# Fixed order for the exponents and sines on ScalarE in a fused attention, feed-forward and expert kernel

## The chip, the cores and the metric

The kernel runs on one core of a Trainium2 chip. The metric is device time in microseconds (us) of one execution, inputs and outputs in HBM. Before the change the median of three runs is 1149.26 us (1148.4 to 1151.08).

## What is computed

Three stages follow each other, all in float32.

```python
# 1. attention: q, k, v are (4, 8, 768, 64); 4 sink columns, window of 128
scores = scale * (q @ k.T); scores = where(is_sink | in_window, scores, -1e9)
a = exp(scores - rowmax); a = a / (rowsum(a) + 1e-9); x = a @ v     # -> (3072, 512)
# 2. feed-forward: w_in (512, 2048), w_out (2048, 512)
h = x @ w_in; g = h * cos(h); x = g @ w_out
# 3. top-1 of 8 experts, 512 -> 1024 -> 512
logits = x @ w_gate + modality_bias[modality_id]; e = argmax(logits)
out[token] = softmax(logits)[e] * (relu(x @ w1[e]) @ w2[e])
```

Stage 1 takes an exponent of every kept score, stage 2 a cosine of every hidden value (made as a sine with a phase of a quarter turn), and the gate of stage 3 a small exponent for every group of tokens. The hidden values are split into a high and a low part for the matrix products, so most products are made of three matmuls.

## The kernel before, in words

The 3072 tokens are eight groups of 384 (`hb` 0 to 7: half a batch item each). Attention of a group goes over four pairs of heads, so there are 32 pairs in all. `attn_front` (L403) loads and transposes q and k of a pair. `mid` (L485) computes its scores in three tiles of 128 rows (`t` 0 to 2), two heads each: matmuls into a PSUM bank `ps`, then a VectorE operation (L516) that masks, copies to `Pb` and leaves the row's maximum in `mx`. After all six blocks stands a loop of six exponents on ScalarE (L529 to L533), one for each tile and head, that read `mx` and leave the row sums in `sm`. `mid` hands back control after every tile of scores, and once more behind the six exponents; between the six it does not. `rest` (L536) normalises the probabilities (on VectorE from `hb` 3 on, on GpSimd in the groups before), transposes them on TensorE (`pt`, L560 to L570), evicts them (`pT`) and multiplies them with v (`po`).

The feed-forward part (`ffn_tile_gen`, from L656) runs one group behind attention, in 128 chunks: 16 blocks of 128 hidden columns for each of eight groups. A chunk is twelve matmuls `hp` (L691 to L693), two VectorE operations that reduce the angle (L142, L145, tile `ch`), one sine on ScalarE (L702), a product with `hp` on VectorE that also frees its PSUM bank (two banks take turns), a copy `g_h` on ScalarE (L712), the low part `g_l` on GpSimd, and two chunks later nine matmuls `y` (L640). `run_ffn` lets chunks pass in step with the weights that the attention part yields; so in the text of the program a few chunks, with their sines, stand between two pairs and between the tiles of scores of one pair. The first group's chunks are divided: six at the start, ten at the very end. Groups 0 and 1 are piped: there a pair's scores and exponents are issued together with the rest of the pair before it. Groups 2 and up issue a pair's scores, its exponents, the next pair's front, and then its rest.

The program text is not the final order. A planner goes over it before the run, with modelled durations, and fixes for each engine one queue: of the instructions that are ready by its model, the one that stands first in the program. Each engine then runs its queue strictly in that order, waiting on semaphores. ScalarE evaluates exponents and sines from tables, and an `ACT_TABLE_LOAD` is put into its queue, after the order is fixed, wherever the next function needs the other table; copies and ReLU need none. The router's exponents (L787, eight of them) are a third user of tables.

After the last chunk the experts run in grids of 256 tokens, with a queue order written out by hand; no exponent or sine is left there. `add_manual_dep(later, earlier, NoSync)` is used in the kernel already for matmuls (`mmf`, L637): it gives the planner an order and puts no semaphore into the program.

Of the kernel before, what the change touches and what calls it, by code (L numbers as in the profile page):

```python
# [16 lines left out]
AF = mybir.ActivationFunctionType  # L17
# [4 lines left out]
TWO_PI = 2.0 * math.pi  # L22
# [39 lines left out]
def kernel(  # L62
# [39 lines left out]
    PE, ACT, DVE, POOL, SP = nc.tensor, nc.scalar, nc.vector, nc.gpsimd, nc.sync  # L102
# [32 lines left out]
    def mm(o, l, r, start, stop):  # L135
        PE.matmul(o, l, r, start=start, stop=stop)  # L136
# [173 lines left out]
        xT[hb] = (xpool.tile([P, NPAIR, HALF], F32R, name="xT_h"), xpool.tile([P, NPAIR, HALF], F32R, name="xT_l"))  # L310

    fronts = {}

    def steps(hb):
        return STEPS_0 if hb <= 1 else STEPS_1
# [80 lines left out]
    def attn_front(hb, pr):  # L396
# [14 lines left out]
        def psb(name):  # L411
            if hb > 0 or not extra:
                return ps_a(name)
            n_ps[0] += 1
            return ps_y(n_ps[0] % NQ, name)
# [67 lines left out]
        mx = sm = Pb = Pt = cols = None  # L483

        def mid():  # L485
            nonlocal mx, sm, Pb, Pt, cols
            kf = [t.rearrange("p t s -> p (t s)") for t in kT]
            klf = [t.rearrange("p t s -> p (t s)") for t in kl] if stack else None
            if extra:
                Pb = [[pb_x[2 * t + j][:, 0:W3] for j in range(2)] for t in range(NQ)]  # L490
            else:
                Pt = late_pool().tile([P, NQ, 2, W3], F32, name="Pb2") if hb >= PB2 and pr % 2 else apool.tile([P, NQ, 2, W3], F32, name="Pb", bufs=PBB)
                Pb = [[Pt[:, t, j] for j in range(2)] for t in range(NQ)]
            mx = apool.tile([P, 2 * NQ], F32, name="mx", bufs=2)
            sm = apool.tile([P, 2 * NQ], F32, name="sm", bufs=2)

            def cols(t):
                if half == 0:
                    return (SEG, W3, 0) if t == 0 else (0, W3, (t - 1) * SEG)
                return 0, W3, t * SEG  # L500

            def scores(t, js):

                c0, c1, o = cols(t)
                w = c1 - c0
                qs = slice(t * P, (t + 1) * P)
                ps = {j: psb("ps") for j in js}
                for j in js:
                    if stack:
                        mm(ps[j][:, 0:w], qT[j][:, qs], kf[j][:, o:o + w], True, False)  # L510
                        mm(ps[j][:, 0:w], qT[j][:, qs], klf[j][:, o:o + w], False, True)
                    else:
                        mm(ps[j][:, 0:w], qT[0][hr[j], qs], kf[0][hr[j], o:o + w], True, True)
                for j in js:
                    i = 2 * t + j
                    DVE.tensor_tensor_reduce(  # L516
                        out=Pb[t][j][:, c0:c1], in0=ps[j][:, 0:w], in1=masks[:, min(half * NQ + t, 2), c0:c1],
                        scale=-SCALE, scalar=3.0e38, op0=ALU.add, op1=ALU.min, accum_out=mx[:, i:i + 1])

            for t in range(NQ):  # L520
                if hb >= PAIRED:
                    scores(t, (0, 1))
                    yield 2 * steps(hb)[1]
                else:
                    for j in range(2):
                        scores(t, (j,))
                        yield steps(hb)[1]
            for t in range(NQ):
                for j in range(2):  # L529
                    c0, c1, _ = cols(t)  # L530
                    i = 2 * t + j
                    ACT.activation(out=Pb[t][j][:, c0:c1], in_=Pb[t][j][:, c0:c1], func=AF.Exp, scale=-1.0,  # L532
                                   bias=mx[:, i:i + 1], accum_out=sm[:, i:i + 1])  # L533
            yield steps(hb)[2]
        def rest():
            xh, xl = xT[hb]  # L536
# [119 lines left out]
    def span(i):  # L656
        return (F0 if i == NTILE else 0), (F0 if i == 0 else NF)
# [4 lines left out]
    def ffn_tile_gen(ypool_of):  # L662
        LAG = 2
        g_t = {}
        yps = {}

        def second(c):
            i, f = seq[c]
            f0, f1 = span(i)
            if f == f0:  # L670
                yps[i] = [ps_y(tt_, f"y{tt_}") for tt_ in range(NQ)]
            gh, gl = g_t.pop(c)
            oh, ol = wo_h[f], wo_l.pop(c)
            for t in range(NQ):
                yp = yps[i][t]
                s = slice(t * P, (t + 1) * P)
                mmf(yp, gh[:, s], oh, f == f0, False)
                mmf(yp, gh[:, s], ol, False, False)
                mmf(yp, gl[:, s], oh, False, f == f1 - 1)
                yield  # L680

        def load_wo(c):
            if c >= F0:
                wo_l[c] = wo_tile()
                SP.dma_start(out=wo_l[c].bitcast(F32), in_=wl_scr[seq[c][1]])

        for c in range(n_all + LAG):
            if c < n_all:
                i, f = seq[c]

                xh, xl = xT[i]  # L691
                hp = ps_h("hp")[:, 0:HALF]
                for p_ in range(NPAIR):  # L693
                    mm(hp, wi_h[f][:, p_, :], xh[:, p_, :], p_ == 0, False)
                    mm(hp, wi_h[f][:, p_, :], xl[:, p_, :], False, False)
                    mm(hp, wi_l[f][:, p_, :], xh[:, p_, :], False, p_ == NPAIR - 1)
                    if p_ < NPAIR - 1:
                        yield c + 0.125 * (p_ + 1)
                ch = mpool.tile([P, HALF], F32, name="ch", bufs=CHB)
                ts(DVE, ch.bitcast(I32), hp, 1.0 / TWO_PI, ALU.mult, 0.25, ALU.add)  # L700
                stt(DVE, ch, hp, 1.0 / TWO_PI, ch.bitcast(I32), ALU.mult, ALU.subtract)
                ACT.activation(out=ch, in_=ch, func=AF.Sin, scale=TWO_PI, bias=half_pi)  # L702
                yield c + 0.5
            if c >= LAG:
                for n_, _ in enumerate(second(c - LAG)):
                    if n_ < NQ - 1:
                        yield c + 0.5 + (n_ + 1) / 6.0
            if c < n_all:
                tt(DVE, ch, ch, hp, ALU.mult)
                gh = mpool.tile([P, HALF], F32R, name="g_h", bufs=GB)  # L710
                gl = mpool.tile([P, HALF], F32R, name="g_l", bufs=GB)
                ACT.activation(out=gh, in_=ch, func=AF.Copy)  # L712
                tt(POOL, gl, ch, gh.bitcast(F32), ALU.subtract)
                g_t[c] = (gh, gl)
                load_wo(c)
            if c == n_all + LAG - 3:
                for r_ in routes:
                    for _ in r_:
                        pass
                routes.clear()  # L720
                ysb[NTILE] = [ypool_of().tile([P, YC], F32, name="yt", bufs=NQ) for _ in range(NQ)]
                for t in range(NQ):
                    SP.dma_start(out=ysb[NTILE][t][:, 0:DM], in_=yp_scr[t])
            i, f = seq[c - LAG] if c >= LAG else (0, -1)
            if f == span(i)[1] - 1:
                if i == 0:

                    for t in range(NQ):
                        yt = mpool.tile([P, DM], F32, name="y_part", tag="wo_l", bufs=WL_BUFS)
                        ACT.activation(out=yt, in_=yps[0][t], func=AF.Copy)  # L730
                        SP.dma_start(out=yp_scr[t], in_=yt)
                elif i == NTILE:
                    for t in range(NQ):
                        yt = ysb[i][t][:, 0:DM]
                        tt(DVE, yt, yps[i][t], yt, ALU.add)
                    ysb[0] = ysb.pop(NTILE)
                    routes.append(route_tile(0, ypool_of()))
                else:
                    ysb[i] = []
                    for t in range(NQ):  # L740
                        yt = ypool_of().tile([P, YC], F32, name="yt", bufs=NQ)
                        ACT.activation(out=yt[:, 0:DM], in_=yps[i][t], func=AF.Copy)
                        ysb[i].append(yt)
                    routes.append(route_tile(i, ypool_of()))
            yield c + 1.0
# [90 lines left out]
    cst = ExitStack()  # L836
    cpool = cst.enter_context(tc.tile_pool(name="cpool", bufs=1))
    conv = conv_gen(cpool)
    ypl = {}
    late_st = ExitStack()  # L840

# [9 lines left out]
    def late_pool():  # L851
        ypool_of()
        return ypl["late"]
# [43 lines left out]
    prow, half_pi = cols2[:, 0:1], cols2[:, 1:2]  # L897
# [149 lines left out]
    for nm in ("xT_h", "xT_l"):  # L1047
        t = xpool.tile([P, KD, 256], F32R, name="m_" + nm, tag=nm)
# [354 lines left out]
```

## Time and profile before

| | |
|---|---|
| runs | 1149.26 us median (1148.4, 1149.26, 1151.08) |
| the profiled execution | 1149.4 us, of which the traced span is 1147.6 us |
| instructions | 20806 |
| groups 0 and 1, attention almost alone | 0 to about 65 us |
| feed-forward and attention together | about 65 to 680 us |
| feed-forward alone | about 680 to 825 us |
| experts | about 825 us to the end |

The traced span begins with the first instruction and ends with the last; 1.8 us of the execution lie around it. An engine is busy where one of its instructions runs; register, branch, semaphore and DMA-issuing instructions don't count. PE is TensorE's matmuls, PEld its weight loads, which run beside matmuls, DVE is VectorE, ACT ScalarE, POOL GpSimd. Matmuls overlap in the pipeline, so a busy PE is not PE at its peak, and a wait of less than the pipeline's depth doesn't show as idle time.

### The profile page before, as it was taken

What the parts mean: (1) busy time and instruction counts of PE and PEld (TensorE: products, weight loads), DVE (VectorE), ACT (ScalarE), POOL (GpSimd) and SP (SyncE); (2) the same over time, 40 slices, a digit from 0 to 9 for tenths busy, and PEclk for the clock granted to TensorE, in tenths of its full rate; (3) what the DMA queues carried; (4) which work ended last, traced back from release to release, by engine and by line L of the source; (5) the groups of instructions that cost most, each with busy time, mean ns of one, the idle gap of its engine ahead of it and who ended that gap; (6) DMA issues with size and microseconds to landing.
All of it is one profiled execution on the core that took longest, in us unless ns stands there. A gap on an engine that the chain in (4) does not pass through costs nothing.

```text
span 1147.6 us, 20806 instructions
## 1 busy us (share of the span) xinstructions
PE 1093.7 (95%) x6504; PEld 936.0 (82%) x6504; DVE 716.4 (62%) x2206; ACT 629.4 (55%) x1283; POOL 224.8 (20%) x275
## 2 busy tenths in 40 slices
PE   5989999999999999999999999999999998999995
PEld 3667677888888888878888889899889997899994
DVE  6678888877876877886788774746741225622210
ACT  4878887766676676666777553434222225522221
POOL 1232224211111111111111112321112211121110
PEclk9999999999999999999999999999999999999998
DMA  6566666433333433433253223723151115111110
GB/s 149 139 193 197 195 200 168 113 86 84 95 91 83 118 82 75 112 86 83 72 118 96 69 78 107 251 62 111 47 193 53 61 39 184 33 62 41 39 42 24
DMA packets 139286, 118.56 MB, mean 103 GB/s; under 512 B 96367, under 2 KB 105583, under 8 KB 139120
## 3 DMA queue, kind: packets, MB, share of 16 engines
q1 hardware_dynamic: 134800, 103.02, 32.3%
q0 software_dynamic: 4320, 13.65, 3.6%
q8 instruction: 65, 1.06, 0.4%
q14 instruction: 101, 0.83, 0.2%
HBM read 151.06 MB, written 19.67 MB: 149 GB/s over the span
## 4 chain that ended last, share of the span: by engine, by line
PE 76%; DVE 12%; ACT 4%; DMA 4%; issue 2%; POOL 1%; SPq 0%; DVEq 0%; POOLq 0%; ACTq 0%
PE hp L136 19%; PE y L640 18%; PE m_y L136 10%; PE m_h L136 10%; PE po L136 5%; PE ps L136 4%; DMA out_dram<-m_ot,m_ids 3%; PE pl L768 1%; DVE pT L148 1%; DVE qT L148 1%; DVE ch L142 1%; DVE kl L148 1%; PE m_a L1107 1%; PE pq L445 1%; PE pt L570 1%
## 5 line engine op out<-in xcount | busy, mean ns | idle before, releaser
L148 POOL TENSOR_TENSOR g_l<-ch,g_h 128x384 fp32r<-128x384 f32 x128 | 133.4, 1043 | 552.9 <-ACT g_h L712 497.6
L136 PE MATMUL hp<-xT_h,wi_h 128*128 128x384 f32 x512 | 182.2, 356 | 2.7 <-DVE ch L148 2.7
L136 PE MATMUL hp<-xT_l,wi_h 128*128 128x384 f32 x512 | 174.7, 341 | 0.0
L136 PE MATMUL hp<-xT_h,wi_l 128*128 128x384 f32 x512 | 174.1, 340 | 0.0
L640 PE MATMUL y<-wo,g_h 128*128 128x512 f32 x384 | 157.2, 411 | 0.0
L640 PE MATMUL y<-wo_l,g_h 128*128 128x512 f32 x384 | 156.0, 406 | 0.0
L640 PE MATMUL y<-wo,g_l 128*128 128x512 f32 x384 | 154.6, 403 | 0.2 <-POOL g_l L148 0.2
L702 ACT ACTIVATE ch<-ch,cols 128x384 f32<-128x384 f32 x128 | 78.9, 617 | 119.4 <-DVE ch L145 117.6
L136 PE MATMUL m_y<-wi_h,hT 128*128 128x512 f32 x416 | 132.5, 393 | 0.7 <-ACT m_ot L1149 0.5
L145 DVE SCALAR_TENSOR_TENSOR hT<-m_h,hT 128x256 fp32r<-128x256 f32 x88 | 37.4, 425 | 151.9 <-ACTq L1301 94.9
L136 PEld LDWEIGHTS hp<-xT_h,wi_h 128*128 128x128 f32 x512 | 96.8, 189 | 10.7 <-issue 3.4
L136 PEld LDWEIGHTS hp<-xT_l,wi_h 128*128 128x128 f32 x512 | 96.9, 189 | 5.5 <-issue 1.9
L142 DVE TENSOR_SCALAR ch<-hp 128x384 int32<-128x384 f32 x128 | 71.0, 555 | 48.0 <-PE hp L136 36.2
L136 PEld LDWEIGHTS hp<-xT_h,wi_l 128*128 128x128 f32 x512 | 96.5, 189 | 1.2 <-issue 0.9
L712 ACT ACTIVATE g_h<-ch 128x384 fp32r<-128x384 f32 x128 | 66.5, 521 | 54.1 <-DVE ch L148 42.9
L148 DVE TENSOR_TENSOR ch<-ch,hp 128x384 f32<-128x384 f32 x128 | 70.4, 550 | 38.3 <-ACT ch L702 37.9
L136 PEld LDWEIGHTS m_y<-wi_h,hT 128*128 128x128 f32 x416 | 78.0, 188 | 16.9 <-issue 0.9
L532 ACT ACTIVATE Pb<-Pb,mx 128x272 f32<-128x272 f32 (+1 forms) x168 | 83.0, 496 | 9.3 <-DVE mx L516 8.4
L640 PEld LDWEIGHTS y<-wo,g_l 128*128 128x128 f32 x384 | 72.3, 188 | 14.2 <-POOL g_l L148 0.8
L1118 ACT ACTIVATE hT<-m_h 128x256 fp32r<-128x256 f32 x88 | 34.0, 387 | 88.0 <-PE m_h L136 80.9
L136 PE MATMUL m_y<-wi_l,hT 128*128 128x512 f32 x208 | 81.0, 389 | 0.0
L640 PEld LDWEIGHTS y<-wo,g_h 128*128 128x128 f32 x384 | 72.4, 189 | 10.5 <-issue 2.7
(280 smaller groups left out, 2368.1 us busy)
## 6 DMA issues: line engine op xcount, KB each, us to landing
rw<-in_moe_w_dram SPq DMA_DIRECT2D x112, 512.0 KB
wo_l<-wl_scr SPq DMA_DIRECT2D x122, 256.0 KB
cv_in<-in_moe_w_in_dram SPq DMA_DIRECT2D x16, 512.0 KB
cv_out<-in_moe_w_out_dram SPq DMA_DIRECT2D x16, 512.0 KB
y_scr<-yt SPq DMA_DIRECT2D x24, 256.5 KB
xT_h<-xg_h SPq DMA_DIRECT2D x32, 192.0 KB
xT_l<-xg_l SPq DMA_DIRECT2D x32, 192.0 KB
qn<-in_q_dram SPq DMA_DIRECT2D x56, 96.0 KB
```

The costliest lines, as they stand in the source:

```text
L136: PE.matmul(o, l, r, start=start, stop=stop)
L142: e.tensor_scalar(out=o, in0=i, scalar1=s1, scalar2=s2, op0=op0, op1=op1)
L145: e.scalar_tensor_tensor(out=o, in0=i0, scalar=s, in1=i1, op0=op0, op1=op1)
L148: e.tensor_tensor(out=o, in0=a, in1=b, op=op)
L445: PE.transpose(pq[:, t * P:(t + 1) * P], qn[:, t].rearrange("p j d -> p (j d)"), ident)
L532: ACT.activation(out=Pb[t][j][:, c0:c1], in_=Pb[t][j][:, c0:c1], func=AF.Exp, scale=-1.0, bias=mx[:, i:i + 1], accum_out=sm[:, i:i + 1])
L570: PE.transpose(pt[:, j, P:2 * P], Pb[t][j][:, SEG:W3], ident)
L640: i = PE.matmul(o, l, r, start=start, stop=stop)
L702: ACT.activation(out=ch, in_=ch, func=AF.Sin, scale=TWO_PI, bias=half_pi)
L712: ACT.activation(out=gh, in_=ch, func=AF.Copy)
L768: return PE.matmul(pl[0][:, 0:NE], yT[:, c, :], wg[:, c, :], start=c == 0, stop=c == KD - 1)
L1118: ACT.activation(out=hT_h[f], in_=hp, func=AF.Relu)
```

## The change

Each exponent of a pair (L532) and each sine (L702) is given an order edge to the one of them that was issued before it in the program. So the planner keeps them in one row, as the program has them: all six exponents of a pair next to each other, as far as these two functions are concerned, and the sines of the chunks in between where the program has them. Copies, ReLUs and the router's exponents are not in the row and may still be placed anywhere. No semaphore, no instruction and no tile is added.

```diff
     fronts = {}
+    row = [None]
+
+    def in_row(i):
+        if row[0] is not None:
+            tc.add_manual_dep(i.ins, row[0].ins.name, in_order, reason="exponents and sines in the order given")
+        row[0] = i
...
-                    ACT.activation(out=Pb[t][j][:, c0:c1], in_=Pb[t][j][:, c0:c1], func=AF.Exp, scale=-1.0,
-                                   bias=mx[:, i:i + 1], accum_out=sm[:, i:i + 1])
+                    in_row(ACT.activation(out=Pb[t][j][:, c0:c1], in_=Pb[t][j][:, c0:c1], func=AF.Exp, scale=-1.0,
+                                          bias=mx[:, i:i + 1], accum_out=sm[:, i:i + 1]))
...
-                ACT.activation(out=ch, in_=ch, func=AF.Sin, scale=TWO_PI, bias=half_pi)
+                in_row(ACT.activation(out=ch, in_=ch, func=AF.Sin, scale=TWO_PI, bias=half_pi))
...
     conv = conv_gen(cpool)
+    in_order = mybir.DependencyInfo(mybir.DependencyClass.NoSync, mybir.DependencyReason.DATA)
```

## Rows read from the trace of the kernel before

**Rows 1.** Page, part 1: busy us, share of the span, instructions of each engine.
```profile
PE 1093.7 (95%) x6504; PEld 936.0 (82%) x6504; DVE 716.4 (62%) x2206; ACT 629.4 (55%) x1283; POOL 224.8 (20%) x275
```

**Rows 2.** Stretches: width, busy us (instructions) of PE, PEld, DVE, ACT, POOL; clock; DMA.
```profile
65.00:110.00 45.00, 41.85 (x266) 31.45 (x267) 34.72 (x81) 37.89 (x81) 14.18 (x30) 0.96 0.66 189
110.00:680.00 570.00, 555.07 (x3269) 469.76 (x3268) 452.17 (x1419) 401.71 (x789) 112.03 (x125) 1.00 0.41 107
680.00:825.00 145.00, 144.31 (x811) 129.96 (x811) 87.09 (x242) 54.99 (x96) 32.69 (x31) 1.00 0.35 112
```

**Rows 3.** ACT's groups: line, operation, count | busy us, mean ns | idle before, releaser.
```profile
L702 ACT ACT_TABLE_LOAD x52 | 66.7, 1283 | 0.9
L532 ACT ACT_TABLE_LOAD x44 | 56.5, 1283 | 0.8
L787 ACT ACT_TABLE_LOAD x8 | 10.3, 1283 | 0.1
L262 ACT ACT_TABLE_LOAD x1 | 1.3, 1283 | 0.7 <-PEq L1382 0.7
```

**Rows 4.** PE's waits from 110 to 680 us: total us, times, longest.
```profile
PE pt L560 <- DVE pT L148: 3.3, 6, 0.6
...
PE pt L560 <- ACT pT L572: 1.6, 3, 0.6
...
PE pz L592 <- POOL kl L451: 0.2, 1, 0.2
```

**Rows 5.** ACT's timeline, pair 14: start us, duration us, instruction [idle before].
```profile
236.26 1.28 ACT L532 ACT_TABLE_LOAD   x1
237.56 0.53 ACT L532 ACTIVATE Pb<-Pb,mx 128x272 f32<-128x272 f32 x1
238.08 0.51 ACT L532 ACTIVATE Pb<-Pb,mx 128x272 f32<-128x272 f32 x1
...
239.72 1.28 ACT L702 ACT_TABLE_LOAD   x1
241.01 0.62 ACT L702 ACTIVATE ch<-ch,cols 128x384 f32<-128x384 f32 x1
241.65 1.28 ACT L532 ACT_TABLE_LOAD   x1
...
243.46 0.51 ACT L532 ACTIVATE Pb<-Pb,mx 128x272 f32<-128x272 f32 x1
243.88 0.19 ACT L532 ACTIVATION_READ_ACCUMULATOR Pb<-Pb,mx 128x1 f32 x1
```

**Rows 6.** DVE's timeline, pair 14: the angle and the last maximum.
```profile
238.98 0.56 DVE L145 SCALAR_TENSOR_TENSOR ch<-hp,ch 128x384 f32<-128x384 f32 x1
...
240.17 0.08 DVE L516 DVE_READ_ACCUMULATOR2_ANT mx<- 128x1 f32 x1
```

**Rows 7.** PE's timeline behind a split (pair 14) and an unsplit group (pair 18).
```profile
248.84 0.41 PE L560 MATMUL pt<-ident,Pb 128*128 128x128 f32 x2 [0.47 <-DVE pT L148]
...
342.62 0.41 PE L570 MATMUL pt<-ident,Pb 128*128 128x128 f32 x2 [0.17 <-DVE qT L148]
```

**Rows 8.** ACT's timeline, pair 18: the last exponent, then the sine that waits.
```profile
337.00 0.19 ACT L532 ACTIVATION_READ_ACCUMULATOR Pb<-Pb,mx 128x1 f32 x1
337.21 1.28 ACT L702 ACT_TABLE_LOAD   x1
```

**Rows 9.** DVE's timeline, pair 18: the angle of that sine.
```profile
337.37 0.55 DVE L145 SCALAR_TENSOR_TENSOR ch<-hp,ch 128x384 f32<-128x384 f32 x1
```

**Rows 10.** ACT's timeline around the first sine.
```profile
65.16 1.28 ACT L702 ACT_TABLE_LOAD   x1
66.45 1.12 ACT L702 ACTIVATE ch<-ch,cols 128x384 f32<-128x384 f32 x2
```

**Rows 11.** PE's timeline: first matmul behind that sine; first use of pair 6's exponents.
```profile
67.71 0.44 PE L136 MATMUL hp<-xT_h,wi_h 128*128 128x384 f32 x1 [2.73 <-DVE ch L148]
...
80.88 0.33 PE L569 MATMUL pt<-ident,pb_x 128*128 128x128 f32 x1
```

## The prediction

> **What bounds the kernel now.** I read the page's first part, then the busy time by stretch, then who waits for whom, and only then timelines. TensorE is the busiest engine, with its weight loads at 82% of the span, VectorE stands at 62% and ScalarE at 55% [rows 1]. ScalarE's share hides a table bill: 105 table loads of 1.283 us, together 134.8 us of its 629.4 [rows 1, 3]. By stretch, feed-forward alone (680 to 825 us) leaves TensorE idle for 0.7 us, so nothing there can be won. From 65 to 110 us it is idle for 3.15 us, from 110 to 680 us for 570 - 555.07 = 14.9 us, while ScalarE is busy for 84% and 70% of these [rows 2]. Everything that this change can win lies in those 18 us of idle time, and in delays too short to show as idle. Of the 14.9 us, 27 waits of over 0.15 us are named, nearly all of them of one kind: TensorE reaches the transposes `pt` (or `pz`, `po`) of a pair before the engines that prepare them are done [rows 4]. They sum to 14.05 us.
>
> **Why exponents and sines matter to these waits.** Of pair 14 the timeline shows what "split" means: a load, four exponents, a load, one sine, a load, two exponents [rows 5]. I laid all exponents and sines of the trace out in the order in which the program issues them. In each of pairs 9 to 32 one sine stands ahead of the six exponents in the program and runs behind some of them in the trace: the planner saw the exponents ready first and had no price for the two extra loads. In 21 of these 24 pairs the sine splits the group (pair 14 is one), in three (11, 18, 26) it comes behind all six. The 24 waits that follow split groups sum to 13.3 us, 0.63 us a pair; the two behind unsplit ones to 0.34 us, 0.11 us a pair (one of each stands in [rows 7]). A group's exponents can also be late because of VectorE, so this is a comparison of few cases, not a proof.
>
> **The change part by part.**
>
> *Loads.* In program order there are 28 runs of exponents and 28 of sines, which take turns. Three of the router's eight exponents stand beside a run of exponents, four among sines (two loads each), and one is last (one load): 28 + 28 + 8 + 1 = 65 loads, if the router's stay where they are. That takes 40 x 1.283 = 51.3 us from ScalarE [rows 3], which is not on TensorE's path as such. In the timeline the load costs its 1.28 us and nothing more: the sine begins 0.01 us behind its load, and the next load 0.02 us behind the sine [rows 5]. The Trainium skill (ScalarE: Activation LUTs, What ACT_TABLE_LOAD costs) adds a drain of about 1380 ns to each switch. By that figure the three loads of a split group would take about 8.0 us instead of 3.9, an estimate by the page, and the recovery below would go to its far end, 1138.5 us. The trace disagrees with the drain, as the 0.01 us shows.
>
> *The sine comes first.* This is what the change adds, and it is a wait. The sine of pair 14 is ready at 238.98 + 0.56 = 239.54 us, 0.71 us before the last maximum at 240.25 [rows 6]. Today four exponents run while ScalarE waits for it. With the edges all six queue behind it, and behind them on ScalarE whatever copies the planner puts there (`qT`, `kT`, `g_h`, `pT`), for which TensorE and VectorE wait. The table holds sines at that point, so the sine needs no load: it ends 0.04 + 0.62 us after 239.54, at 240.20; the load ends at 241.50; six exponents at steps of 0.51 us and a last one of 0.61 with its read end at 244.65 [rows 5]. Today the last read ends at 243.88 + 0.19 = 244.07. So the sixth exponent is not earlier, it is 0.58 us later, and the first, at 241.51 instead of 237.56, is 3.95 us later. Worked alike for all 21 split pairs it is 0.55 us later on the mean (from 2.1 us earlier to 1.6 us later). For the three unsplit ones it is worse: pair 18's last read ended at 337.19, its sine is ready at 337.92 [rows 8, 9], and 337.92 + 5.1 is 5.8 us later, or 5.6 with its two narrow exponents.
>
> *Why this can still win.* What stalls TensorE is not that exponents are late but that they are later than the planner's order assumes. In the model the loads are free, so today's order puts the transposes some 3 x 1.28 = 3.85 us too early behind a split group. With the edges the model itself sees the wait for the sine and moves the transposes back by up to four exponents, 2.0 us, with feed-forward matmuls ahead of them, while the chip is 0.55 us later. One load stays unpriced before the sixth exponent: the mismatch falls by 2 x 1.28 = 2.57 us. That is the state of the unsplit groups with their 0.11 us. The far end of the gain is therefore 21 x (0.63 - 0.11) = 10.9 us. The near end is nothing: VectorE's normalisation of the first two tiles moves behind the sine too and can meet the next pair's work there. Since the tied groups have the loads of the unsplit ones but the lateness of the split ones, I take the middle, 5.5 us, which is a choice between two sets of rows that lie equally near.
>
> *The first stretch.* The first sine ran at 66.45 us behind pair 6's exponents and a load that began at 65.16 [rows 10]; TensorE stood for 2.73 us until the bank of its `hp` was free [rows 11]. In the program this sine stands ahead of pair 6. Its load would then be over long before, which is worth up to 1.3 us of the 2.73. Pair 6's exponents move behind it, but are first used at 80.88 [rows 11], so they cost nothing. Two other things happen: the third sine, which ran well ahead of pair 7's exponents, must wait for them, and the stretch 65 to 110 us gets seven loads instead of five, 2.6 us more on ScalarE, whose idle time there is 45 - 37.89 = 7.1 us [rows 2]. The bounds are -1.3 and +2.6; I take 0, as the nearest row, the idle 7.1 us, covers the added loads.
>
> *Nothing else.* There is no new semaphore or byte. Before 65 us only exponents are in the row, and they already run in order but for two swaps. From 680 us on the loads hide under a full TensorE [rows 2]; the expert stage has none.
>
> **The sum.** 1149.4 (the profiled execution: span 1147.6 and 1.8 around it) - 5.5 + 0 = 1143.9. The median of the runs shown lies 0.14 us below that execution, so I put 1143.8.
>
> **The rivals.**
>
> *ScalarE's time is hidden anyway.* TensorE has the work, ScalarE is idle for 30% of 110 to 680 us, and the waits behind `pt` come from VectorE's crowding at the same place (the largest named releaser is VectorE's `pT`, 3.3 us [rows 4]). Then the 51 us vanish into ScalarE's idle time, and the time stays within 1 us of 1149.3. For it: the sixth exponent is not earlier. Against: 0.63 beside 0.11. The Trainium skill (Perfetto Trace Analysis, Identifying the Most-Contended Engine) says to work on the engine with the highest occupancy first, and by that rule, with which the trace's shares agree, this is the outcome.
>
> *Slower: the sine holds up the exponents.* The place is the head of ScalarE's queue in pairs 9 to 32, the price the lateness worked out above, 0.55 us for each of 21 pairs, 11.6 us, if TensorE's order does not give way; half of it, 5.8 us, if it gives way by half. That is 1155.1 to 1161.0; I put it at 1155.1. It decides from the point where TensorE's idle time is above 0.63 us a pair. For it: the three unsplit pairs get 5.6 us later each, and the copies behind the exponents are held too. Against: the planner does price the sine's wait.
>
> *The gain is whole.* Both the 10.9 us and the 1.3 us of the first stretch come: 1137.1.
>
> *It does not do what it says.* The new order shifts the router's exponents and other copies so that loads stay near 105, or the first stretch pays its 2.6 us: 1149 to 1152.
>
> **How the numbers follow.** The forecast has 0.45, hidden anyway 0.24, slower 0.20, the whole gain 0.06, no effect or the first stretch's price 0.05. A measurement of this kernel tells about 0.2%, 2.3 us, from no change. Faster by more takes 0.43 of the forecast and the whole gain: 0.49. Within 0.2% takes 0.02 of the forecast, 0.24, and 0.02 of the last: 0.28. Slower: 0.20 + 0.03 = 0.23. The forecast's own range is 1138.5 (10.9 us) to 1149. The range goes from 1138 to 1156: below lies the whole gain, above the fuller prices of the slower case, less than 2 in 10 together.
>
> **What would show it.** Right: about 65 loads on ScalarE, 28 each of L532 and L702 plus a few; no sine inside a group; the sixth exponent about as late behind its maximum as now or later, but TensorE's idle time from 110 to 680 us near 9 us and its `pt` waits halved; ScalarE's busy time near 578 us. Wrong: idle time unchanged at 15 us with 40 loads fewer (hidden anyway), or above 20 us with the waits behind exponents or `sm` (slower); a longer wait than 2.73 us near 67 us would mean the first stretch was misread.

## The result and the profile after

The changed kernel takes 1161.31 us (median of four runs, 1158.65 to 1164.83) against 1149.98 us for the kernel before (four runs, 1148.4 to 1151.08). The ratio is 1.0099, with an interval of 1.0082 to 1.0116: 11.3 us slower, where 5.5 us faster was forecast.

The engines' busy time after, as in [rows 1]:

```profile
PE 1101.7 (95%) x6504; PEld 938.3 (81%) x6504; DVE 719.8 (62%) x2206; ACT 579.4 (50%) x1249; POOL 226.2 (19%) x275
```

ScalarE lost 50.0 of its 629.4 us, almost what was forecast, and the kernel is slower all the same. The stretches of [rows 2], after (width, busy us and instructions of PE, PEld, DVE, ACT, POOL, then the clock and the DMA share):

```profile
65.00:110.00 45.00, 41.23 (x264) 30.87 (x265) 33.53 (x79) 43.18 (x94) 13.73 (x30) 1.00 0.65 182
110.00:680.00 570.00, 549.12 (x3205) 458.99 (x3202) 445.30 (x1365) 339.25 (x732) 111.31 (x124) 1.00 0.39 105
680.00:825.00 145.00, 144.21 (x779) 128.92 (x778) 91.40 (x262) 61.52 (x109) 33.98 (x33) 1.00 0.38 120
```

TensorE's idle time from 110 to 680 us rose from 14.9 to 570 - 549.12 = 20.9 us, and ScalarE's busy time from 65 to 110 us from 37.89 to 43.18 us. The loads by line, as in [rows 3] (count | busy us, mean ns | idle before):

```profile
L708 ACT ACT_TABLE_LOAD x35 | 44.9, 1283 | 0.6
L538 ACT ACT_TABLE_LOAD x27 | 34.6, 1283 | 0.5
L793 ACT ACT_TABLE_LOAD x8 | 10.3, 1283 | 0.1
```

With the first one of all, 71 loads instead of 105. TensorE's largest waits from 110 to 680 us, as in [rows 4] (total us, times, longest):

```profile
PE pt L566 <- DVE kl L148: 2.7, 4, 0.7
PE pt L566 <- ACT pT L578: 2.3, 2, 1.2
PE pt L566 <- DVE yT L765: 2.1, 3, 0.7
PE pt L566 <- DVE sm L140: 2.0, 3, 0.7
```

The named waits grew from 14.05 us in 27 to 20.0 us in 32. They are still waits of a pair's transposes, and a releaser is there that none of the waits before names: `sm`, VectorE's normalisation, which stands behind the exponents.

Now one pair closely. Pair 14 on ScalarE, to be laid beside [rows 5] (start us, duration us, instruction, idle before):

```profile
243.76 0.62 ACT L708 ACTIVATE ch<-ch,cols 128x384 f32<-128x384 f32 x1 [3.99 <-DVE ch L145]
244.40 1.28 ACT L538 ACT_TABLE_LOAD   x1
245.69 0.53 ACT L538 ACTIVATE Pb<-Pb,mx 128x272 f32<-128x272 f32 x1
...
248.65 0.19 ACT L538 ACTIVATION_READ_ACCUMULATOR Pb<-Pb,mx 128x1 f32 x1
```

and on VectorE, beside [rows 6]:

```profile
243.17 0.56 DVE L145 SCALAR_TENSOR_TENSOR ch<-hp,ch 128x384 f32<-128x384 f32 x1
244.36 0.08 DVE L522 DVE_READ_ACCUMULATOR2_ANT mx<- 128x1 f32 x1
...
247.46 0.17 DVE L148 TENSOR_TENSOR lg<-pl,bias_all 128x8 f32<-128x8 f32 x1 [2.10 <-PE pl L774]
247.54 0.16 DVE L140 TENSOR_SCALAR sm<-sm 128x2 f32<-128x2 f32 x1
...
252.62 0.14 DVE L140 TENSOR_SCALAR sm<-sm 128x2 f32<-128x2 f32 x1
```

The last two lines begin the pair's first and third normalisation. Before, these were

```profile
240.67 0.17 DVE L140 TENSOR_SCALAR sm<-sm 128x2 f32<-128x2 f32 x1
...
245.16 0.43 DVE L140 TENSOR_SCALAR sm<-sm 128x2 f32<-128x2 f32 x1
```

ScalarE stands for 3.99 us until VectorE hands over the angle of one sine, with all six exponents queued behind it; before, four of them ran ahead of the sine. So the pair's first normalisation comes 3.10 us behind its last maximum, where it came 0.42 us behind it before, and the third 8.2 us, where it was 4.9. (VectorE also runs dry for 2.10 us just ahead of it. The profile names TensorE's `pl`, a product of the router, as what it waited for, so this wait is not shown to be the exponents'.) TensorE, beside [rows 7], then waits for the normalisation:

```profile
252.77 0.30 PE L566 MATMUL pt<-ident,Pb 128*128 128x128 f32 x1 [0.68 <-DVE sm L140]
```

It was 0.47 us before, with another releaser. The same over a whole period: the traces repeat every eight pairs, so pairs 13 to 20 stand for 13 to 32. The sixth exponent's end (without its read) is in us behind the pair's last maximum. Columns are those of feed-forward matmuls (384 for an `hp`, 512 for a `y`) between the pair's last scores and its first or last transpose `pt`: a measure of TensorE's order that does not depend on waits. "Waits" is the sum of TensorE's waits of over 0.15 us, and "length" the time, from this pair's last maximum to the next pair's, in us.

| pair | sixth exponent, before | after | first `pt`, columns before | after | last `pt`, before | after | waits, before | after | length, before | after |
|---|---|---|---|---|---|---|---|---|---|---|
| 13 | 3.45 | 4.31 | 10752 | 10752 | 20608 | 20096 | 0.49 | 0.70 | 23.33 | 24.03 |
| 14 | 3.72 | 4.30 | 12288 | 12288 | 18944 | 19968 | 0.47 | 0.68 | 24.74 | 25.15 |
| 15 | 3.42 | 3.81 | 12288 | 12288 | 18944 | 18944 | 0.63 | 0.60 | 25.18 | 25.26 |
| 16 | 3.70 | 4.73 | 12288 | 14208 | 20480 | 25344 | 1.02 | 1.23 | 24.26 | 24.88 |
| 17 | 3.59 | 4.43 | 10752 | 12288 | 19968 | 19456 | 1.13 | 1.56 | 21.96 | 22.02 |
| 18 | 0.71 | 6.51 | 12544 | 20352 | 16128 | 23296 | 0.17 | 0.72 | 21.11 | 22.74 |
| 19 | 2.54 | 2.78 | 10368 | 10368 | 17920 | 17408 | 0.66 | 0.68 | 23.24 | 22.53 |
| 20 | 2.72 | 4.07 | 10752 | 10752 | 18432 | 18944 | 0.00 | 0.67 | 27.29 | 28.12 |
| mean, 13 to 31 | 3.03 | 4.33 | | | | | 0.57 | 0.84 | 23.98 | 24.41 |

A pair takes 0.43 us longer; 0.27 of that are named waits. The first transposes stand at the same place of TensorE's order in five of the eight pairs, the last ones within 1024 columns of their old place in six.

Finally the time by stage, from the last `y` matmul of a chunk in each trace. (Pairs are counted from 1 here; groups and chunks from 0, in the quoted expectations too.) Chunk 5 ends 0.1 us later than before, chunk 21, the end of group 1's chunks, 3.8 us later, chunk 98 11.8, and the last one, 127, 11.9. So there are two losses: **3.6 us early**, between chunks 5 and 21, and **8.0 us late**, between 21 and 98, which is the attention of groups 3 to 7. The feed-forward stretch behind it is unchanged, as forecast. The profiled execution was the longest of the four, and its expert stage, which the change does not touch, holds 3.3 us more than before's (its granted clock is 0.97 there, against 0.98 before); so I go by stages, not by spans.

The two losses are not of one kind. From the end of chunk 5 to that of chunk 21 TensorE runs the same matmuls in both kernels; before, then after:

```profile
125.47:222.41 96.94, 93.93 (x514) 74.10 (x513) 81.22 (x221) 76.71 (x154) 32.38 (x47) 1.00 0.59 170
```

```profile
125.61:226.19 100.58, 97.07 (x514) 74.63 (x513) 82.03 (x220) 67.30 (x148) 30.76 (x46) 1.00 0.57 167
```

Its idle time grows by 0.5 us there and its busy time by 3.1 us, at the same clock. Waits too short to show as idle would look like this; which ones they are is not shown. Of the late 8.0 us, 5.1 are idle time.

The 0.1 us at chunk 5 hides something too. From 65 to 110 us the granted clock was 0.96 before [rows 2] and is 1.00 after, which is 0.04 x 45 = 1.8 us in favour of the change. The kernel e6 below has the queues of before up to chunk 5, at a clock of 1.00, and ends that chunk 2.1 us earlier than before. At the same clock, then, the change is about 2 us late at chunk 5 already, by one trace of each.

### The profile page after: what moved, and what is told of

The parts are those of the page before. It is cut to its first block, busy times and chain, and to the rows that moved or that the text cites. A ratio compares the mean times of both kernels' runs of the same rounds, so it can differ in the third digit from the quotient of the medians.

```text
span 1162.8 us, 20786 instructions
## 1 busy us (share of the span) xinstructions
PE 1101.7 (95%) x6504; PEld 938.3 (81%) x6504; DVE 719.8 (62%) x2206; ACT 579.4 (50%) x1249; POOL 226.2 (19%) x275
## 5 line engine op out<-in xcount | busy, mean ns | idle before, releaser
L522 DVE CUSTOM_DVE_ANT_0 Pb<-ps,masks 128x272 f32<-128x272 f32 (+1 forms) x168 | 64.2, 411 | 27.8 <-PE ps L136 27.5
L646 PEld LDWEIGHTS y<-wo_l,g_h 128*128 128x128 f32 x384 | 72.5, 189 | 10.0 <-issue 1.9
```

Of the source, the lines that this page charges most:

```text
L522: DVE.tensor_tensor_reduce(out=Pb[t][j][:, c0:c1], in0=ps[j][:, 0:w], in1=masks[:, min(half * NQ + t, 2), c0:c1], scale=-SCALE, scalar=3.0 ...
L646: i = PE.matmul(o, l, r, start=start, stop=stop)
```

## The experiments

Theory at the start: the six exponents queue behind a sine that waits for VectorE, so the normalisation and the transposes come late. Rival A: the planner's order in general got worse by being tied, whichever side of the exponents the sine is on. Rival B: the loads, or ScalarE's time, are what counts. The ten kernels, with before and after, in one table. "Early" and "late" are the lengths of the two stages in us, "lag" the mean of the sixth exponent behind the last maximum (pairs 13 to 32), "idle" TensorE's from 226 to 680 us, "loads" those of the late stage.

| kernel | ratio, interval | early | late | lag | idle | loads |
|---|---|---|---|---|---|---|
| before | 1 | 96.9 | 459.7 | 3.07 | 11.0 | 76 |
| after | 1.0099, 1.0082 to 1.0116 | 100.6 | 467.6 | 4.35 | 16.5 | 48 |
| e1_group_first | 1.0008, 0.9993 to 1.0023 | 101.7 | 456.2 | 0.70 | 8.1 | 42 |
| e2_but_three | 1.0078, 1.006 to 1.0096 | 99.8 | 466.2 | 3.76 | 15.3 | 48 |
| e3_one_table_before | 1.0112, 1.0092 to 1.0131 | 93.7 | 464.6 | 0.83 | 14.6 | 0 |
| e4_one_table_after | 1.0123, 1.0098 to 1.0148 | 98.7 | 467.2 | 2.92 | 15.7 | 0 |
| e5_group_first_from_3 | 0.9974, 0.9963 to 0.9986 | 96.5 | 456.3 | 0.70 | 8.3 | 42 |
| e6_row_from_3 | 1.0069, 1.0049 to 1.0089 | 96.6 | 467.4 | 4.34 | 15.7 | 48 |
| e7_exponents_only | 1.0071, 1.0056 to 1.0087 | 103.0 | 459.5 | 3.06 | 11.3 | 76 |
| e8_third_table | 1.001, 0.9998 to 1.0022 | 96.8 | 459.6 | 3.06 | 10.9 | 76 |
| e9_row_from_1 | 1.0143, 1.0127 to 1.0159 | 100.0 | 467.8 | 4.34 | 16.7 | 48 |
| e10_row_early | 1.0034, 1.0021 to 1.0047 | 100.7 | 459.4 | 3.06 | 11.3 | 76 |

The ratios are of medians of several executions; the other columns come from one trace of each kernel. e8, whose queues are those of before, shows how well a stage repeats: to 0.1 us. The ends do not: its chunk 5 ends 2.1 us later than before's, at a granted clock of 0.93 from 65 to 110 us against 0.96, and the expert stage takes 334.3 to 337.8 us in these twelve traces. At the end of chunk 5 only e3 (9.9 us late), e9 (4.0) and e4 (2.7) are more than 2.3 us from before's, which the two columns do not hold.

**The group ahead of the sine.** The kernel before, with the opposite edge: the sine that the program gives ahead of a pair's exponents must come behind all six.

```diff
+            if last_sine[0] is not None and hb >= 2:
+                tc.add_manual_dep(last_sine[0].ins, e_.ins.name, in_order, reason="the group first")
+                last_sine[0] = None
...
-                ACT.activation(out=ch, in_=ch, func=AF.Sin, scale=TWO_PI, bias=half_pi)
+                last_sine[0] = ACT.activation(out=ch, in_=ch, func=AF.Sin, scale=TWO_PI, bias=half_pi)
```

> One load for a group of exponents, as after the change, but the exponents don't wait: from group 2 on, the last sine issued before a pair's exponents is put behind its sixth exponent. If exponents late behind the sine are what costs (theory 1), the sixth exponent ends about 1 us behind its maximum instead of 4.3, and the time goes back to that of before or below: 1140 to 1150 us. If the saved loads let TensorE's order down (theory 2: the fewer loads, the more the queue orders are off), it stays near 1161 us. If any new order costs (theory 3), 1152 to 1162 us.

1151.75 us against 1150.2: no difference that can be told, and just above what theory 1 allowed. But the lag is 0.70 us, as expected, and the stages differ: the late one is 3.4 us shorter than before and 11.4 shorter than after, with fewer loads still, and the loss is all ahead of chunk 21. So tying as such is not what costs late (against rival A); which side the sine is on is.

**All pairs but three.** The change, but the row is cut ahead of the exponents of pairs 11, 18 and 26, in which before the sine ran behind all six.

```diff
+            if (hb, pr) in ((2, 2), (4, 1), (6, 1)):
+                row[0] = None
```

> The kernel after the change, but three pairs (11, 18, 26), whose exponents ran ahead of the sine before and are 6 to 11 us later after, are let out of the row: their sine may run behind them again. Theory 1: the two steps of about 3 us at pairs 17 to 19 and 25 to 27 shrink by 2 us or more each, 1154 to 1158 us. Theories 2 and 3: nothing changes, 1160 to 1163 us.

1159.68 us, less given back than the 1154 to 1158 us of theory 1. Pair 18 is as before again (sixth exponent 0.70 us behind the last maximum, first `pt` 6.23 us behind it), and the late stage is 1.5 us shorter than after: 0.7 us for each of pairs 18 and 26. The direction is the theory's, but a lateness of 5.8 us costs 0.7 us, as TensorE's order has more feed-forward matmuls ahead of that `pt` (20352 columns in the table, against 12544). So 6.5 of the 8.0 us are in the other pairs.

**No loads at all.** The kernel before, and the change, with the sine replaced by an exponent and its bias by zero, so that one table does and the angle's cosine is not computed; first on the kernel before, then on the change.

```diff
-                ACT.activation(out=ch, in_=ch, func=AF.Sin, scale=TWO_PI, bias=half_pi)
+                ACT.activation(out=ch, in_=ch, func=AF.Exp, scale=TWO_PI, bias=half_pi)
...
-    DVE.memset(half_pi, HALF_PI)
+    DVE.memset(half_pi, 0.0)
```

> The kernel before, with the sine replaced by an exponent of the same angle and a bias of zero (so the output is not the reference's): one table serves all, 1 load instead of 105. If loads cost as such, because TensorE waits for what stands behind them, this is faster than before by up to 11 us up to the end of the feed-forward stage; if ScalarE's time is hidden, within 2 us of before there. The expert stage may differ, since the tokens fall to other experts.

> The kernel after the change with the same replacement: one table, 1 load instead of 71, exponents still in the row behind the sine. Theory 1: slower than the one-table kernel before by 5 to 12 us at the end of the feed-forward stage, since the wait for the sine stays (sixth exponent some 3 us behind its maximum instead of 1). Theory 2: no difference, since there are no loads left to misjudge. Theory 3: a difference of either sign.

1162.92 and 1163.36 us: both as slow as the change, with one load. Of e3, the page's first part and its only load:

```profile
PE 1100.6 (95%) x6504; PEld 941.3 (81%) x6504; DVE 721.6 (62%) x2206; ACT 499.1 (43%) x1179; POOL 229.2 (20%) x275
```

```profile
L262 ACT ACT_TABLE_LOAD x1 | 1.3, 1283 | 0.7 <-PEq L1382 0.7
```

ScalarE is 130 us less busy than before and the kernel is 1.1% slower. That speaks against rival B. But the pair of runs does not isolate the loads as I meant it to: e3's queues are not before's. At 995 of the 6504 places of TensorE's matmuls in the traces another matmul stands (by tiles and shape), most of e3's loss (9.9 us) lies ahead of chunk 5, and e4 comes out level with e3 where a gap was expected (a difference of 2.6 us is left in the late stage, at a lag of 2.92 against 0.83). Nor do these two fit theory 1 as it stands: e4's exponents come a little less late than before's (2.92 against 3.07 us), and its late stage is 7.5 us longer than before's.

**A third table.** Before, with the sine replaced by a Gelu (the cosine is again not computed): another function, and the same switches.

```diff
-                ACT.activation(out=ch, in_=ch, func=AF.Sin, scale=TWO_PI, bias=half_pi)
+                ACT.activation(out=ch, in_=ch, func=AF.Gelu, scale=TWO_PI, bias=half_pi)
```

> The kernel before with the sine replaced by another function that needs a table of its own (Gelu; the output is not the reference's): loads and dependences are those of before. It is the control of e3: if e3 was slow because of other data or another function, this is slow too up to 825 us (by about 11 us); if e3 was slow because the planner, seeing no loads, laid its queues otherwise, this agrees with before within 2 us there.

1150.71 us, and the queues of TensorE, ScalarE and VectorE are those of before, place for place. So another function by itself re-plans nothing. What did it in e3 is likely the shared table, and then the planner's order depends on the switches; that it times an exponent otherwise than a sine and a Gelu is not excluded by these two runs.

**From group 3 on, either side.** Two kernels that leave everything ahead of group 3 alone: e5 is e1 with `hb >= 3`, e6 is the change with its row from there on.

```diff
-            if last_sine[0] is not None and hb >= 2:
+            if last_sine[0] is not None and hb >= 3:
```

```diff
     def in_row(i):
+        if not (now[0] >= 3):
+            return
...
+        now[0] = hb
```

> The exponents first, as in e1, but only from group 3 on; groups 0 to 2 keep the order of before, where e1 lost 5 us. Theory 1 (only the exponents' lateness costs, and a group that is neither split nor late gains a little): 1144 to 1148 us, with 3 to 4 us won in groups 4 to 7. Theory 3 (any new order costs): 1151 to 1156 us.

> The mirror of e5: from group 3 on the row of the change, so exponents behind the sine; groups 0 to 2 as before. Theory 1: 1155 to 1160 us, 8 to 11 us above e5. Theory 3: about e5's time, since both move a like number of instructions.

e5 takes 1147.13 us against 1149.96, faster than both kernels; e6 takes 1156.38. Both are within what theory 1 expected. Both have before's early stage (96.5 and 96.6 us). They act on the same pairs, with 42 and 48 loads in the late stage. In the traces the order of exponents and sines differs there by one sine a pair, which stands on the other side of the six (and by the router's exponents at three pairs), and the stages are 11.2 us apart. Pair 14 on ScalarE in e5:

```profile
236.53 0.52 ACT L533 ACTIVATE Pb<-Pb,mx 128x272 f32<-128x272 f32 x1
...
239.41 0.51 ACT L533 ACTIVATE Pb<-Pb,mx 128x272 f32<-128x272 f32 x1
239.83 0.19 ACT L533 ACTIVATION_READ_ACCUMULATOR Pb<-Pb,mx 128x1 f32 x1
240.03 1.28 ACT L706 ACT_TABLE_LOAD   x1
241.33 0.62 ACT L706 ACTIVATE ch<-ch,cols 128x384 f32<-128x384 f32 x1
```

and in e6:

```profile
237.58 0.62 ACT L711 ACTIVATE ch<-ch,cols 128x384 f32<-128x384 f32 x1 [4.01 <-DVE ch L145]
...
239.51 0.52 ACT L541 ACTIVATE Pb<-Pb,mx 128x272 f32<-128x272 f32 x1
...
242.05 0.51 ACT L541 ACTIVATE Pb<-Pb,mx 128x272 f32<-128x272 f32 x1
```

The last maximum comes at 239.22 us in e5 and at 238.26 in e6. So the first exponent runs 2.69 us ahead of it in e5 and 1.25 behind it in e6, and the sixth ends 0.70 and 4.30 us behind it. The planner uses this in e5: in five of the eight pairs of the period the last transpose stands 2432 to 4864 columns earlier in TensorE's order than before, and the named waits of a pair fall from 0.57 to 0.41 us. No wait of TensorE for `ch`, which the sine feeds, is named there. The windows from 226 to 680 us say the same of all pairs; before, then after:

```profile
226.00:680.00 454.00, 443.02 (x2663) 381.28 (x2662) 352.58 (x1155) 307.93 (x602) 76.12 (x76) 1.00 0.36 90
```

```profile
226.00:680.00 454.00, 437.48 (x2615) 372.88 (x2614) 348.25 (x1110) 261.16 (x560) 77.29 (x76) 1.00 0.34 88
```

and e5, then e6:

```profile
226.00:680.00 454.00, 445.73 (x2676) 383.56 (x2676) 347.56 (x1160) 264.85 (x567) 77.50 (x77) 1.00 0.34 90
```

```profile
226.00:680.00 454.00, 438.34 (x2623) 374.24 (x2622) 346.91 (x1121) 260.44 (x558) 75.88 (x74) 1.00 0.34 88
```

ScalarE's busy time is nearly equal in the last three (260 to 265 us, 43 to 48 less than before), while TensorE's idle time is 16.5, 8.3 and 15.7 us. Less ScalarE work went with a gain in one and a loss in two, so rival B falls here.

The side of the sine decides, then. By what path it costs time is not settled by these runs. One path is that of theory 1, the late exponents. Another is that ScalarE itself is held: while it stands at a sine, the copies queued behind the sine (`qT`, `kT`, `g_h`, `pT`) wait with the exponents. ScalarE's idle time ahead of sines whose angle VectorE has not made yet, from 226 to 680 us (total us, times, longest), before, after and in e5:

```profile
ACT ch L702 <- DVE ch L145: 72.8, 36, 5.2
ACT ch L708 <- DVE ch L145: 105.2, 41, 5.0
ACT ch L706 <- DVE ch L145: 69.3, 42, 3.3
```

and in e3 and e4, which the lag does not order:

```profile
ACT ch L702 <- DVE ch L145: 98.7, 64, 5.2
ACT ch L708 <- DVE ch L145: 141.0, 61, 5.0
```

The twelve late stages follow this time within 0.4 us, except e4's, which is 0.5 us shorter than after's. (e3 and e4 have no loads that could run during such a wait. Where the loads are counted as waiting, the five are 81, 119, 71, 102 and 146 us, in the same order.) No run here holds the copies and lets the exponents go.

**Exponents alone in the row.** The change without the sines in it, so that 105 loads remain.

```diff
-                in_row(ACT.activation(out=ch, in_=ch, func=AF.Sin, scale=TWO_PI, bias=half_pi))
+                ACT.activation(out=ch, in_=ch, func=AF.Sin, scale=TWO_PI, bias=half_pi)
```

> Only the exponents are in the row, the sines are free to come between them as before; 105 loads, nothing waits that did not wait. It differs from before by two swaps of exponents before 65 us and what follows from them. Theory 1: 1149 to 1152 us, same as before. Theory 3: 1153 us or more.

1157.62 us, where theory 1 expected no difference. The late stage is before's (459.5 us, lag 3.06), so the late loss comes from the sines' edges alone. The whole loss is early: 6.0 us between chunks 5 and 21. Two swaps of exponents near 42 us are all that these edges undo, and 315 of the 6504 places of TensorE's matmuls change with them, all between 45 and 207 us. (The median is 7.7 us up, not 6.0; what the rest is, one trace does not tell.) The stretches from 110 to 226 and from 226 to 680 us:

```profile
110.00:226.00 116.00, 106.80 (x578) 83.30 (x577) 96.57 (x253) 88.01 (x178) 33.73 (x49) 1.00 0.58 169
226.00:680.00 454.00, 442.70 (x2661) 381.04 (x2660) 352.28 (x1146) 309.29 (x604) 76.99 (x76) 1.00 0.34 90
```

TensorE's idle time from 110 to 680 us is 9.2 + 11.3 = 20.5 us, hardly less than the change's 20.9, for another reason and in another place. That one number, which the prediction named as its test, could not have told the two losses apart.

**The early part by itself.** The change with its row only from group 1 on (e9), and only in groups 0 and 1 (e10).

```diff
     def in_row(i):
+        if now[0] < 1:
+            return
```

```diff
     def in_row(i):
+        if not (now[0] < 2):
+            return
```

> The change without its edges among the thirty exponents ahead of the first sine (pairs 1 to 5, which only undo two swaps near 42 us). After e7 the early loss should come from these: then this runs at e6's time, 1155 to 1159 us, and loses nothing up to chunk 21. If the early loss comes from the sines of groups 1 and 2 that wait, it stays near 1161 us.

> The change in groups 0 and 1 alone, nothing tied from group 2 on (107 loads). By chunks, the change lost 3.8 us up to chunk 21 and 7.9 us after: this should lose the first part alone, 1152 to 1155 us, and match before from chunk 21 to 98 within 0.5 us. If the later part needs the early one, it would not add up with e6.

e10 takes 1154.83 us: the early loss alone, with before's late stage (459.4). Its 0.34% and e6's 0.69% add up to 1.03%, beside the change's 0.99%: two separate losses. e9 went against its expectation: 1167.1 us, where leaving group 0 untied was to give the whole early loss back. It is 7.1 us late at chunk 21, 4.0 of that already at chunk 5, part of it at the first wait for an `hp` bank:

```profile
69.26 0.44 PE L136 MATMUL hp<-xT_h,wi_h 128*128 128x384 f32 x1 [3.99 <-DVE ch L148]
```

which was 2.73 us in [rows 11]. So the early loss does not belong to one set of edges that could be left out: that stage is 6.0 us longer with two swaps in group 0 undone (e7), 3.7 with groups 0 and 1 in the row (e10), 3.1 with all but group 0 (e9), and 4.8 with the opposite edges from group 2 on (e1, of which about 1.7 us are its granted clock, 0.98 in that stage against 1.00).

## Why the prediction was wrong

**The bill of loads held.** 71 loads instead of 65, because all eight of the router's exponents got a load of their own, and ScalarE's busy time 579.4 us where 578 was forecast. A load costs 1.28 us and no more in the trace after, too: the first exponent of pair 14 begins 0.01 us behind its load.

**So did the lateness.** The sixth exponent of pair 14 was forecast 0.58 us later and is 0.58 us later (4.30 against 3.72). For the unsplit pair 18 it was 5.6 to 5.8, and is 5.80. The 0.55 us of 21 split pairs and the 5.6 us of three come to 1.18 us on the mean of 24 pairs; measured over pairs 13 to 32, 4.35 - 3.07 = 1.28.

**The step that failed** is "In the model the loads are free", and with it "With the edges the model itself sees the wait for the sine and moves the transposes back". If the order of the kernel before already depends on the switches, as e3 beside e8 makes likely, there was no such mismatch that taking two loads out of a group could remove. What is shown is that the transposes did not move back as a whole: the first of a pair stands where it stood in pairs 13, 14, 15, 19 and 20, the last within 1024 columns of it in six of eight, about 0.5 us at the 0.23 us that a `y` of 512 columns takes where they run back to back. Only in pairs 16 and 18 did it move by more than the 2.0 us of the prediction. In 13 to 15 the steps behind the transposes did move back (pair 14's `pz` by 2304 columns), which helps no transpose. The waits that were to fall to 0.11 us a pair rose from 0.57 to 0.84. The split pairs' 0.63 beside the unsplit ones' 0.11 was read as the price of two loads. The unsplit pairs of before (11, 18, 26) have two things, no load inside the group and a sixth exponent 0.6 to 0.7 us behind the maximum. The change gives every pair the first without the second, and its waits rise: the first alone is not what made 0.11. e5 gives every pair both and wins 3.4 us of the late stage, a third of the far end of 10.9; its waits are 0.41 us a pair, not 0.11, so the comparison of few cases overstated what that state is worth.

**The slower rival had the mechanism and the place**: "the sine holds up the exponents", at the head of ScalarE's queue. I gave it 0.20, and half its price (1155.1 us; 1149.4 + 5.8 is 1155.2), because "the planner does price the sine's wait". Priced or not, the order did not give way in most pairs. Its full price, 1161.0 us, agrees with the 1161.3 measured by chance: it was 0.40 us for each of 20 pairs (8.0 us), not 0.55 for 21, and the rest of the loss comes from elsewhere. It also gave the test that spoke: idle time "above 20 us with the waits behind exponents or `sm`".

**The first stretch** was forecast at 0, between -1.3 and +2.6 us. The first sine's load was to be "over long before" TensorE needs it. In the trace after, ScalarE is still held by the copies `pT` ahead of it, and the second sine (74.66) has pair 6's exponents ahead of it; beside [rows 10]:

```profile
64.23 1.09 ACT L578 ACTIVATE pT<-pt 128x512 f32<-128x512 f32 x2
65.34 1.28 ACT L708 ACT_TABLE_LOAD   x1
66.63 0.62 ACT L708 ACTIVATE ch<-ch,cols 128x384 f32<-128x384 f32 x1
...
74.66 0.62 ACT L708 ACTIVATE ch<-ch,cols 128x384 f32<-128x384 f32 x1
```

and TensorE, beside [rows 11], waits as long as before, and once more for a bank of `hp`:

```profile
67.89 0.45 PE L136 MATMUL hp<-xT_h,wi_h 128*128 128x384 f32 x1 [2.73 <-DVE ch L148]
...
87.69 0.45 PE L136 MATMUL hp<-xT_h,wi_h 128*128 128x384 f32 x1 [0.83 <-DVE ch L148]
```

The working looked at one sine and its load; the copies around it, which no edge ties, stayed where they were. The seven loads came, but ScalarE's busy time there rose by 5.3 us, not 2.6, and at the same clock the change is about 2 us late at chunk 5, near the far end of +2.6. And the working ended at 110 us: the loss of 3.6 us lies between chunks 5 and 21 (125 to 226 us). "Nothing else", on the argument that before 65 us the exponents "already run in order but for two swaps", was wrong as well: e7 undoes the two swaps, ties no sine, and loses 6.0 us between chunks 5 and 21.

**It did what it says**: no sine stands inside a group, with 27 loads at the exponents' line for 32 pairs; that rival and the whole gain fell with the forecast.

**Hidden anyway** was wrong in its number but not in its core: the 51 us did not shorten the kernel. The Trainium skill (ScalarE: Activation LUTs, Table sets: the hidden batching unit) says to batch activations by table set. Both e6 and e5 do that, and their loads in the late stage are 48 and 42; one costs 0.69% and the other wins 0.26%. The runs here agree with the rule as far as the loads go, and show that it leaves open which set goes first, which decided the sign here.

**What stays open.** Which of the changed places costs the early 3.6 us: e7, e9 and e10 show only that edges of either kind in groups 0 to 2 move that stretch, not by which instruction. Whether late exponents or held copies carry the late loss. Why e3, with no loads and a lag of 0.83 us, has a late stage 4.9 us longer than before's: its waits name `yT` behind `kT` (2.8 us) where before has none, and ScalarE stands longer at its sines, which says where and not why. A version with e5's edges and a better early order was not tried.

## What to carry to other kernels

When work on an engine that is not the bottleneck is grouped to save switches, ask first who waits for each member, and put the one that the bottleneck's next step needs at the head of the queue: the same grouping won 2.8 us with the exponents first and lost 6.4 with the sine first. A saving in busy time was worth nothing here by itself. How long the last needed result comes behind its input (here the sixth exponent behind the last maximum) went with the length of the late stage in ten of the twelve kernels here, but not in e3 and e4, which have one table; look also at how long the engine stands at the head of its queue. An order edge without a semaphore is not a local edit where a planner orders all the queues: compare stage by stage, and tie only the stretch in which it helps.

## What the runs showed of the hardware that was not expected

With 130 us of ScalarE's work gone and one table load left, e3 was slower than before by 1.1%. About half of the 9.9 us by which its chunk 5 was late stands in TensorE's granted clock, the third column from the end in its stretches:

```profile
65.00:110.00 45.00, 41.30 (x241) 30.15 (x240) 34.88 (x81) 32.68 (x77) 12.09 (x29) 0.92 0.64 194
110.00:140.00 30.00, 27.43 (x141) 21.14 (x139) 24.05 (x58) 17.74 (x43) 9.96 (x13) 0.89 0.61 178
```

Before, these were 0.96 [rows 2] and 1.00, so 0.04 x 45 + 0.11 x 30 = 5.1 us of full speed were missing. A mean below 1.00 comes from a part of the stretch at the lower level, 0.50 in the traces (1.2 instead of 2.4 GHz). TensorE was idle for 2.6 of the 30 us behind 110 us, against 1.2 before; but e7, idle for 4.2 us there, kept 1.00, so idle time by itself does not order the runs. Nor does one long wait: the clock of before fell at 68.6 us, 0.9 us behind the end of the 2.73 us of [rows 11], and after the change the same wait of 2.73 us was followed by no fall. So the clock costs the change nothing from 65 to 825 us, where it was 1.00; it cost before 1.8 us, and a comparison of the two up to chunk 5 has to take that out.

A load of a third table costs what the sine's costs: in e8 the loads at L702 read as in [rows 3], 52 of 1283 ns, now for the Gelu, and the time is before's within the interval.
